# Agent attention and a mixture of experts on one core: an order set by step numbers replaced by a list scheduler in the kernel

## Chip, cores and metric

One core of a Trainium2 chip. The metric is the device time of one execution in microseconds (us). The kernel before was run twice: 1181.36 and 1184.54, median 1182.95 us.

## The reference

For each of B = 4 batches there are N = 11456 tokens of 128 values and 49 agents. The agents attend to the keys, which gives 49 agent values; each query attends to the agents and mixes these values. The 45824 rows x go through a top-1 mixture of 8 experts.

```python
a2k = softmax(scale * agents @ k.T)          # 49 x N
agent_v = a2k @ v                            # 49 x 128
x = softmax(scale * q @ agents.T) @ agent_v  # N x 128
logits = x @ w_gate                          # 8 experts
e = argmax(logits); gate = softmax(logits)[e]
out = gate * (relu(x @ w1[e]) @ w2[e])       # w1: 128 x 1024, w2: 1024 x 128
```

## The kernel before

A batch has 12 chunks: eleven of 1024 tokens (128 partitions x 8) and one of 192. Values in fp32 are split into an fp16 high and low part, and a product is then three fp16 matmuls.

*Keys* of a chunk: load, sum of squares on ACT (`squares`, L330), a power-of-two scale from its bits with three small DVE operations (`scale_bits`, L211, L215, L218), high part on ACT and low part on DVE (`split`, L346, L348), a DMA transpose from SP (`turn_over`, L370), the scores on PE (L397 to L399), evicted by L413 or L415, and a running maximum (L434). In the first batch the keys are instead transposed by PE in fp32 and scored by fp32 matmuls (`transposed`, L385; L395). After the last chunk come the column maximum (`keymax`, L439 to L451), then per chunk the subtraction (`kexp`, L459), the exponential (L464), its sum on POOL or DVE (`kexp3`, L474) and the product with v (`values`, L487). Small work follows: agent values, the batch's main expert (`choose`), the loads of its two weights, the folding of agent values into the first weight (L700), scales and splits (`weights`). `pow2_scale` (L180) is PE and DVE in turn, emitted at once.

*Queries* of a chunk: the same split, transpose and scores, then maximum, subtraction (L576, L578) and exponential (L583), the exponentials' split into the tile `mm` (L590, L594), a DMA transpose into M (`eturn`, L600), the routing logits (`logits`, L609 to L613) and, for groups of two or three chunks, the routing (`route`, L628 to L655).

*Experts.* All tokens of a batch go through the batch's most likely expert, in 23 groups of up to 512 tokens x 8 slices of 128 hidden values: 184 steps. A step is a first layer (two matmuls of 512 columns, L1171 and L1172), a relu on ACT (L1177), the low part on DVE (L1178), and five steps later (`LAG`) a second layer of twelve matmuls (L1191). The hidden part waits in four PSUM buffers and eight SBUF tiles. Each group is scaled and stored (L1204).

*Leftovers.* Tokens of other experts are ranked (`leftover_ranks`, on POOL, in the last batch on DVE), gathered by indirect DMAs into 14 blocks of 128 (`prepare_blocks`), and run with their own weights after the last batch (`block_layer1`, `block_layer2`). `weight_squares` (L884) loads all 16 expert weights for their scales. A loop behind that would run blocks that are still left.

*What orders the work.* A heap of events. Each function is put at a time in units of expert steps, by constants at the top (L45 to L64): `at(t, f)` and `after(dt, f)`. Steps of the experts stand at 184 b + i. The events are taken in order of time and each emits what its function holds, for all engines it uses:

```python
at(base + t + kl, kscores, c)
at(base + tl, logits, c)
after(NDL, weight_squares2, j, x)        # the square, 4 steps behind its load
```

Keys of the next batch start at step -208 of that batch, ten steps apart, its values four steps apart, and its queries at -20, 8 to 13 steps apart; so both overlap in the first part of a batch. Loads are issued three uses ahead (`AHEAD`). An engine takes its instructions in the order emitted, so each of them can hold up what stands behind it. `hold` (L919) makes a small tile on DVE that the next relu takes as its bias (L1175).

## Time and profile before

| | |
|---|---|
| median of 2 runs | 1182.95 us |
| profiled execution, its own time | 1182.58 us |
| its span, first to last instruction | 1180.9 us |
| PE busy | 1049.1 us (89%) |
| PE weight loads busy (beside PE) | 839.2 us (71%) |
| DVE busy | 981.8 us (83%) |
| ACT busy | 754.1 us (64%) |
| POOL busy | 142.2 us (12%) |
| granted TensorE clock, mean | 0.952 |

PE is the matmul engine, DVE the vector engine, ACT the scalar engine, POOL is GpSimd and SP only issues DMAs. L12 is line 12 of the kernel. A granted clock of 1 is 2.4 GHz, of 0.5 is 1.2 GHz. "<-" behind an idle time names what ended it; "issue" means that nothing in the profile did.

### The profile page before, as it was taken

To read this page: it belongs to the slowest core of one execution; us is meant where nothing else is said; L and a number is where in the kernel's file an instruction comes from. 1 tells how busy PE (TensorE), PEld (TensorE's weight loads), DVE (VectorE), ACT (ScalarE), POOL (GpSimd) and SP (SyncE) were. 2 spreads that over 40 slices of the span, in tenths; PEclk is the share of its full clock that TensorE was granted. 3 is DMA by queue.
4 is the path that set the end of the run, shared out by engine and by line. 5 is a ranking of instruction groups with operands and counts; after the bars stand their busy time and mean duration, and the time that the engine had idled before them with its cause. 6 is when DMAs were issued, how large, how long until landed. Compare 5 with 4: busy or idle time off the path is not lost.

```text
span 1180.9 us, 34788 instructions
## 1 busy us (share of the span) xinstructions
PE 1049.1 (89%) x14206; PEld 839.2 (71%) x14206; DVE 981.8 (83%) x2442; ACT 754.1 (64%) x1338; POOL 142.2 (12%) x193
## 2 busy tenths in 40 slices
PE   8747799899998899799988989899989789999995
PEld 8726577677776777677776768677767677667895
DVE  3668899797788999698787999697789798799985
ACT  4548785574486886574486777574576556666682
POOL 0200000043000000042100000042000112110123
PEclk9858899999998999899998999999999999899998
DMA  8599988631299899741399998741365545423270
GB/s 328 208 208 244 226 201 209 162 110 47 85 266 210 184 234 226 190 118 41 100 263 220 179 230 204 179 102 49 108 166 117 117 101 133 142 79 130 66 273 14
DMA packets 265666, 190.94 MB, mean 162 GB/s; under 512 B 217513, under 2 KB 230306, under 8 KB 265504
## 3 DMA queue, kind: packets, MB, share of 16 engines
q1 hardware_dynamic: 263648, 185.39, 61.6%
q0 software_dynamic: 1568, 2.25, 1.1%
q8 instruction: 112, 1.84, 0.6%
q10 hardware_dynamic: 288, 1.05, 0.3%
q14 instruction: 50, 0.41, 0.1%
HBM read 99.75 MB, written 36.43 MB: 115 GB/s over the span
## 4 chain that ended last, share of the span: by engine, by line
PE 24%; DVE 17%; issue 7%; DMA 7%; ACT 5%; POOL 2%; POOLq 0%; SPq 0%; ACTq 0%; DVEq 0%
PE py L1191 11%; DVE hh L1178 7%; PE ph L1171 4%; PE ph L1172 4%; DMA M<-mm 3%; DMA ld<-in_q_dram 2%; ACT hh L1177 2%; DMA wn<-in_moe_w_dram 1%; POOL out_dram L1073 1%; DVE S L459 1%; PE ps_small L487 1%; ACT jk L330 1%; DVE wsp L1032 1%; DVE yo L1204 1%; DVE hl L348 1%
## 5 line engine op out<-in xcount | busy, mean ns | idle before, releaser
L1191 PEld LDWEIGHTS <-hh 128*128 128x128 f16 x8640 | 554.8, 100 | 174.0 <-issue 12.7
L1191 PE MATMUL py<-w2h,hh 128*128 128x128 f16 (+1 forms) x5760 | 614.4, 221 | 3.2 <-DVE E L578 2.2
L1177 ACT ACTIVATE hh<-ph 128x512 f16<-128x512 f32 (+1 forms) x728 | 414.4, 585 | 252.7 <-PE ph L1172 232.2
L1178 DVE SCALAR_TENSOR_TENSOR hh<-ph,hh 128x512 f16<-128x512 f32 (+1 forms) x736 | 482.4, 669 | 87.7 <-ACT hh L1177 83.2
L1191 PE MATMUL py<-w2l,hh 128*128 128x128 f16 (+1 forms) x2880 | 529.9, 221 | 0.9 <-issue 0.9
L1171 PE MATMUL ph<-M,Ah 128*128 128x512 f16 (+1 forms) x736 | 282.2, 384 | 27.4 <-DVE hh L1178 21.0
L1172 PE MATMUL ph<-M,Al 128*128 128x512 f16 (+1 forms) x736 | 281.5, 383 | 0.2 <-issue 0.2
L348 DVE SCALAR_TENSOR_TENSOR hl<-ld,mul,hl 128x1024 f16<-128x1024 f32 (+1 forms) x84 | 102.3, 1219 | 3.8 <-ACT hl L346 3.3
L346 ACT ACTIVATE hl<-ld,mul 128x1024 f16<-128x1024 f32 (+1 forms) x84 | 91.2, 1092 | 10.1 <-DVE mul L215 9.9
L1172 PEld LDWEIGHTS <-Al 128*128 128x128 f16 x736 | 73.1, 99 | 31.3 <-issue 30.6
L330 ACT ACTIVATE jk<-ld 128x1024 f16<-128x1024 f32 (+1 forms) x84 | 84.7, 1008 | 14.6 <-DMA ld<-in_q_dram 11.5
L1171 PEld LDWEIGHTS <-Ah 128*128 128x128 f16 x736 | 74.2, 101 | 12.0 <-issue 9.4
L594 POOL TENSOR_TENSOR mm<-E,mm 128x392 f16<-128x392 f32 (+1 forms) x18 | 18.2, 1011 | 527.0 <-DVE mm L590 494.9
L397 PE MATMUL ps_s<-agh,hT 128*128 128x49 f16 x572 | 54.8, 187 | 14.7 <-DMA hT<-hl 10.1
L397 PEld LDWEIGHTS <-hT 128*128 128x128 f16 (+1 forms) x630 | 53.6, 99 | 17.4 <-DMA hT<-hl 14.7
L1204 DVE TENSOR_TENSOR yo<-py,cs 128x512 f32<-128x512 f32 (+1 forms) x92 | 61.4, 668 | 2.3 <-PE ps_s L609 2.3
L398 PEld LDWEIGHTS <-hT 128*128 128x128 f16 (+1 forms) x630 | 52.6, 99 | 5.0 <-issue 4.4
L398 PE MATMUL ps_s<-agl,hT 128*128 128x49 f16 x572 | 54.4, 186 | 0.3 <-DVE agl L319 0.3
L399 PE MATMUL ps_s<-agh,hT 128*128 128x49 f16 x572 | 54.2, 186 | 0.0
L399 PEld LDWEIGHTS <-hT 128*128 128x128 f16 (+1 forms) x630 | 52.2, 99 | 0.5 <-issue 0.4
L583 ACT ACTIVATE E<-E,ln,div 128x392 f32<-128x392 f32 (+1 forms) x48 | 33.3, 694 | 26.1 <-DVE E L578 25.1
L474 POOL TENSOR_TENSOR es<-es,S 128x392 f32<-128x392 f32 (+1 forms) x39 | 42.5, 1091 | 23.3 <-ACT S L464 16.6
(296 smaller groups left out, 1253.3 us busy)
## 6 DMA issues: line engine op xcount, KB each, us to landing
ld<-in_k_dram SPq DMA_DIRECT2D x44, 512.0 KB
ld<-in_v_dram SPq DMA_DIRECT2D x44, 512.0 KB
ld<-in_q_dram SPq DMA_DIRECT2D x44, 512.0 KB
out_dram<-yo SPq DMA_DIRECT2D x88, 256.0 KB
w1e<-in_moe_w_dram SPq DMA_DIRECT2D x17, 512.0 KB
w2e<-in_moe_w_dram SPq DMA_DIRECT2D x17, 512.0 KB
exps<-E SPq DMA_DIRECT2D x44, 196.0 KB
wn<-in_moe_w_dram SPq DMA_DIRECT2D x16, 512.0 KB
```

The source lines that it names most:

```text
L330: nc.scalar.activation(jk[:p, :t * D], x[:p, :t, :].rearrange("p t d -> p (t d)"), AF.Square, accum_out=ss[:p])
L346: nc.scalar.activation(hi[:p, :t, :], x[:p, :t, :], AF.Copy, scale=m)
L348: nc.vector.scalar_tensor_tensor(lo[:p, :t, :], x[:p, :t, :], m, hi[:p, :t, :], op0=ALU.mult, op1=ALU.subtract)
L397: nc.tensor.matmul(o, x[:, 0, i, :p], AG["h"], start=True, stop=False)
L398: nc.tensor.matmul(o, x[:, 0, i, :p], AG["l"], start=False, stop=False)
L399: nc.tensor.matmul(o, x[:, 1, i, :p], AG["h"], start=False, stop=True)
L1171: nc.tensor.matmul(ph[:, :nn], st['Ah'][:, f, :], m, start=True, stop=False)
L1172: nc.tensor.matmul(ph[:, :nn], st['Al'][:, f, :], m, start=False, stop=True)
L1177: nc.scalar.activation(hh[:, 0, :nn], ph[:, :nn], AF.Relu)
L1178: nc.vector.scalar_tensor_tensor(hh[:, 1, :nn], ph[:, :nn], 0.0, hh[:, 0, :nn], op0=ALU.max, op1=ALU.subtract)
L1191: mm_ = lambda l, r, **k: nc.tensor.matmul(o, l, r, skip_group_check=True, **k)
L1204: nc.vector.tensor_tensor(yo[:p, :n, :], py[:p, :n * D].rearrange("p (i d) -> p i d", d=D), cs.unsqueeze(2).broadcast_to([p, n, D]), op=AL ...
```

## The change

Every piece of work becomes an entry for one engine, with a rank (its old step number, roughly), a cost in us, the entries that it needs, and the buffers that it takes and frees. `Plan.order` walks a clock over PE, DVE, ACT, POOL and SP: whenever an engine is free, the entry with the lowest rank whose needs are done and whose buffers are free goes next. DMAs go through one modelled queue (`move`) and land after `land`. Pools in `strict` are taken in order of rank. DVE entries other than those of experts and blocks get 8 added to their rank. The order that comes out is emitted as it is.

Beside it: of a chunk's scale, the first operation stays on DVE and the two others go to POOL; the sums of two logits become one reduction; routing has 12 DVE operations instead of 14; in the first batch every second key chunk is scaled by one power of two for all its partitions and scored in fp16; 13 load buffers instead of 11, 4 split tiles instead of 6; the weights to be squared go into load buffers, ten steps ahead; 2 query chunks instead of 3 are made before the first experts; the first batch's exponentials are summed on DVE but for the first; the held tiles are gone. The arithmetic of experts and blocks is unchanged.

```diff
-LDB, HLB, SPB, MP, HP, NH, NY = 11, 6, 14, 6, 8, 4, 2
+LDB, HLB, SPB, MP, HP, NH, NY = 13, 4, 14, 6, 8, 4, 2
...
+class Plan:
+    LATE = dict(DVE=0.12, ACT=0.14, PE=0.1, POOL=0.14, SP=0.1)
...
+        while len(out) < len(self.all):
+            while future and future[0][0] <= t + 1e-9:
+                e = heapq.heappop(future)[2]
+                ready[e["eng"]].append(e)
+            did, soon = False, float("inf")
+            for g in engines:
+                if busy[g] > t + 1e-9:
+                    continue
+                best = None
+                for e in ready[g]:
+                    when = can(e, t)
...
+                    if best is None or (e["rank"], e["n"]) < (best["rank"], best["n"]):
+                        best = e
...
+                busy[g] = t + e["cost"]
+                end = t + e["cost"] + (0.0 if e["move"] else self.LATE[g])
+                if e["move"]:
+                    begin = max(t + 0.4 * e["cost"], queue[0])
+                    queue[0] = begin + e["move"]
+                    end = max(end, queue[0]) + e["land"]
...
+        def scales(src, c):
+            p, hb = P if uniform(src, c) else chunks[c][1], SC[src, c]
+            mul = two.tile([P, 1], F32, tag="s" + src + "m", name="mul", bufs=6)
+            nc.gpsimd.tensor_scalar(mul[:p].bitcast(I32), hb[:p], -1.0, float(204 << 23), op0=ALU.mult, op1=ALU.add)
+            div = two.tile([P, 1], F32, tag="s" + src + "d", name="div", bufs=6)
+            nc.gpsimd.tensor_scalar(div[:p].bitcast(I32), hb[:p], AG["bits"][:p, :1], None, op0=ALU.add)
...
+            m = SC[src, c][0][:, :1]
+            if eng == "A":
...
+                nc.scalar.activation(TT[src, c][:, 0, h:h + n, :p], pv, AF.Copy, scale=m)
+            else:
...
+                nc.vector.scalar_tensor_tensor(xT[:, 1, h:h + n, :p], pv, m, xT[:, 0, h:h + n, :p],
+                                               op0=ALU.mult, op1=ALU.subtract)
...
-            lg = two.tile([P, 8, E + 1], F32, tag="lg", name="lg")
-            pv = ps[:p, :t * E2].rearrange("p (t e) -> p t e", e=E2)
-            nc.vector.tensor_copy(lg[:p, :t, :], pv[:, :, E + 1:])
-            nc.vector.tensor_tensor(RT["L"][:p, c * 8:c * 8 + t, :], pv[:, :, :E + 1], lg[:p, :t, :], op=ALU.add)
+            pv = QP.pop(c)[:p, :t * E2].rearrange("p (t j e) -> p t e j", j=2, e=E + 1)
+            nc.vector.tensor_reduce(RT["L"][:p, c * 8:c * 8 + t, :], pv, axis=AX.X, op=ALU.add)
...
-            nc.vector.tensor_scalar(se, d, 0.0, float(E), op0=ALU.is_lt, op1=ALU.mult)
-            nc.vector.tensor_tensor(se, se, eb, op=ALU.add)
-            yield
-            nc.vector.tensor_reduce(lm, se, axis=AX.X, op=ALU.min)
+            nc.vector.scalar_tensor_tensor(se, d, 0.0, eb, op0=ALU.is_ge, op1=ALU.mult)
+            nc.vector.tensor_reduce(lm, se, axis=AX.X, op=ALU.max)
...
-            nc.vector.tensor_scalar(rk, rk, 1e-9, None, op0=ALU.add)
-            nc.vector.reciprocal(rk, rk)
-            nc.vector.tensor_tensor(g, g, rk, op=ALU.mult)
+            nc.vector.scalar_tensor_tensor(g, rk, 1e-9, g, op0=ALU.add, op1=ALU.mult)
+            nc.vector.reciprocal(g, g)
...
+            add(n_("scaling", *x), base + t + d[1], "POOL", 0.33, scales, *x, r=[n_("hb", *x)],
+                take=[("sc" + src, n_(*x))])
+            add(n_("upper", *x), base + t + d[2], "ACT", 1.0 * u + 0.1, upper, *x, r=[n_("scaling", *x)], take=[("hl", n_(*x))])
+            add(n_("lower", *x), base + t + d[3], "DVE", 1.15 * u + 0.1, lower, *x, r=[n_("upper", *x)], free=[("ld", n_(*x))])
+            add(n_("turn", *x), base + t + d[4], "SP", 2.9 if u == 1 else 2.4, turn_over, *x, r=[n_("lower", *x)], take=[("hT" + src, n_(*x))],
+                free=[("hl", n_(*x))], land=1.3, move=3.0 if u == 1 else 0.8)
...
+            add(n_("kexp", c), base + t, "DVE", 0.5, kexp, c, r=[n_("keymax", 4)], head=None if first else head(t - HEAD))
...
+                    (eturn, 10, "SP", 1.25, None, dict(take=[("M", n_("q", c))], free=[(m_, n_("q", c))], land=1.3, move=1.5))):
...
+            add(n_("logits", c), base + tl, "PE", 0.22, logits, c, r=[n_("eturn", c), av(10)], take=[("s", n_("l", c))])
...
+                add(("L1", i), i, "PE", 0.432 * u, layer1, g, f, r=[(b, "eturn", c), (b, "fl", 0), (b, "fl", 1), ("L1", i - 1) if i else None],
+                    take=[("H", ("h", i))], free=([("M", (b, "q", c))] if lastc else []) + ([("W", (b, "A"))] if last_ else []))
+                add(("up", i), i + 0.3, "ACT", 0.49 * u, upper, g, f, r=[("L1", i)], take=[("hh", i)])
+                add(("lo", i), i + 0.6, "DVE", 0.6 * u + 0.02, lower, g, f, r=[("up", i)], free=[("H", ("h", i))])
+                add(("L2", i), i + LAG + 0.5, "PE", 0.67 * u, layer2, g, f, r=[("lo", i), (b, "sl"), ("L2", i - 1) if i else None], free=[("hh", i)],
+                    take=[("Y", (b, g))] if f == 0 else [])
...
+        add(("wn", j), t - 10, "SP", 0.4, weight_squares, j, take=[("ld", ("wn", j))], land=2.2, move=1.3, head=("L1", t - 14))
+        add(("wn2", j), t, "ACT", 1.3, weight_squares2, j, r=[("wn", j)], free=[("ld", ("wn", j))])
...
+    with tc.manual_schedule():
+        for e in plan.order():
+            e["f"](*e["a"])
```

## Rows read from the trace of the kernel before

**Rows 1.** Windows by stage: us, busy (x instructions) per engine, PEclk, DMA share, GB/s.
```profile
0.00:85.00 85.00, 57.26 (x555) 52.70 (x555) 46.49 (x141) 38.06 (x68) 9.76 (x24) 0.80 0.78 249
85.00:359.50 274.50, 247.21 (x3377) 193.38 (x3378) 230.66 (x557) 185.17 (x327) 26.04 (x42) 0.94 0.71 173
359.50:622.20 262.70, 241.29 (x3373) 189.91 (x3370) 225.59 (x544) 178.90 (x316) 28.45 (x43) 0.97 0.73 174
622.20:882.10 259.90, 237.47 (x3317) 186.66 (x3314) 222.69 (x537) 172.68 (x304) 29.01 (x42) 0.98 0.67 159
882.10:1122.10 240.00, 221.51 (x2885) 173.36 (x2882) 215.70 (x601) 147.28 (x275) 30.24 (x28) 0.98 0.43 112
1122.10:1180.90 58.80, 44.34 (x719) 43.15 (x717) 40.68 (x67) 32.04 (x51) 18.66 (x14) 0.94 0.42 143
```

**Rows 2.** First line of the first layer: durations min/median/max ns, first and last start.
```profile
L1171 PE MATMUL ph<-M,Ah x736: 242/379/634, 85.0 to 1122.1; 128*128 128x512 f16 x176, 128*128 128x192 f16 x8
```

**Rows 3.** Chain that ended last: start us, us, what.
```profile
456.26 0.67 PE py L1191 x12
457.36 0.67 PE py L1191 x12
...
655.88 6.36 DMA M<-mm
```

**Rows 4.** Waits, whole span: waited for, us in total, times, longest us.
```profile
ACT jk L895 <- DMA wn<-in_moe_w_dram: 26.9, 11, 6.0
...
PE ph L1171 <- DVE hh L1178: 21.0, 15, 3.9
...
PE ps_s L609 <- DMA M<-mm: 20.1, 11, 3.6
...
PE ps_s L397 <- DMA hT<-hl: 10.1, 8, 1.8
...
PE ps_small L190 <- DVE pdg L188: 7.2, 6, 3.2
...
PE ps_small L442 <- DVE m L439: 7.1, 4, 2.6
```

**Rows 5.** Timeline, a stall in the second batch: start us, us [idle before <-releaser].
```profile
479.94 10.18 SPq L890 DMA_DIRECT2D wn<-in_moe_w_dram  x3
...
483.73 1.06 ACT L895 ACTIVATE jk<-wn 128x1024 f16<-128x1024 f32 x1 [6.05 <-DMA wn<-in_moe_w_dram]
...
485.40 2.48 DVE L1178 SCALAR_TENSOR_TENSOR hh<-ph,hh 128x512 f16<-128x512 f32 x4 [6.99 <-ACT hh L1177]
486.14 0.58 PE L1171 MATMUL ph<-M,Ah 128*128 128x512 f16 x1 [3.89 <-DVE hh L1178]
```

**Rows 6.** Groups by form: xcount, busy us, mean ns, idle before.
```profile
L218 DVE TENSOR_SCALAR div<-hb,bits 128x1 int32<-128x1 int32 x77 | 15.5, 203 | 0.0
...
L215 DVE TENSOR_SCALAR mul<-hb 128x1 int32<-128x1 int32 x81 | 11.8, 145 | 0.4
...
L612 DVE COPY lg<-ps_s 128x72 f32<-128x72 f32 x39 | 8.7, 223 | 6.9 <-PE ps_s L609 6.9
...
L820 POOL TENSOR_TENSOR cp<-cp,C 128x8 f32<-128x8 f32 x36 | 7.4, 206 | 2.8
```

**Rows 7.** Source of a routing line: min/median/max ns.
```profile
L631 DVE TENSOR_SCALAR sel<-Ld x20: 185/243/424, 85.0 to 1047.6; 128x192 f32<-128x192 f32 x8, 128x64 f32<-128x64 f32 x4, 128x128 f32<-128x128 f32 x4, 128x144 f32<-128x144 f32 x4
```

**Rows 8.** Groups by form: key scores of the first batch, fp32.
```profile
L395 PE MATMUL ps_y<-agf,xT 128*128 128x49 f32 x96 | 12.0, 280 | 0.0
...
L395 PE MATMUL ps_s<-agf,xT 128*128 128x49 f32 x80 | 9.4, 271 | 0.0
```

**Rows 9.** Timeline of PE over one fp16 score chunk, first matmul and what follows.
```profile
453.96 0.19 PE L397 MATMUL ps_s<-agh,hT 128*128 128x49 f16 x1
...
454.57 0.38 PE L1171 MATMUL ph<-M,Ah 128*128 128x512 f16 x1
```

**Rows 10.** Source of the key subtraction: min/median/max ns.
```profile
L459 DVE TENSOR_TENSOR S<-S,mxb x48: 246/594/1385, 41.4 to 786.0; 128x392 f32<-128x392 f32 x44, 96x98 f32<-96x98 f32 x4
```

More of the change, by code (lines that the diff above doesn't have):

```diff
@@ L426, in kmax @@
             sv = S[c][:p, :t, :]
-            if PKM and not first:
-                return
             if c == 0:
@@ new lines, in attention @@
+        add(n_("agload"), base + (KS - 20 if not first else -400) if b != 1 else base - steps - 8, "SP", 0.4, agent_load, land=1.5, move=0.1,
+            take=[("ag", n_())], head=head((KS if b > 1 else KS1 - base) - 14) if not first else None)
+        ka = -400 if first else KS - 8 if b > 1 else KS1 - base - 6
+        add(n_("agscaled"), base + ka, "DVE", 0.3, agent_scaled, r=[n_("agload")])
+        add(n_("agsquares"), base + ka + 0.1, "ACT", 0.5, agent_squares, r=[n_("agscaled")])
+        add(n_("agsum"), base + ka + 0.2, "PE", 0.4, agent_sum, r=[n_("agsquares")], take=[("s", n_("ag"))], free=[("ag", n_())])
@@ L1008, in prepare_blocks @@
         nc.vector.tensor_tensor(gt, gt, div[:, :n], op=ALU.mult)
+        yield
         for i in range(n):
```

1045 lines of the change are left out of this document (663 added, 382 removed).

## Prediction

> **What bounds the kernel now.** I read the windows by stage first, then the groups for the price of one piece of work, then the waits for what breaks the pace, then one break in the timeline.
>
> The first expert matmul starts at 85.0 us, the last at 1122.1 [rows 2]. So there are three stages: a head of 85 us, a steady part of 1037.1 us with 736 expert steps in four batches, and a tail of 58.8 us with the 14 leftover blocks. In the steady part PE is busy for 247.2 + 241.3 + 237.5 + 221.5 = 947.5 us and idle for 89.6 [rows 1]. DVE is busy for 230.7 + 225.6 + 222.7 + 215.7 = 894.7 us, that is 86%. Two engines are thus both near the limit. Undisturbed, a step costs 1.10 us: the twelve second-layer matmuls of one step start at 456.26, those of the next at 457.36, back to back [rows 3]. So PE sets the pace where nothing breaks it.
>
> Two things break it. One is the 89.6 us of PE idle time. The other is the granted clock: it averages 0.94, 0.97, 0.98 and 0.98 over the four batches [rows 1], and since its levels are 1 and 0.5, the half-speed time is 2 x (0.06 x 274.5 + 0.03 x 262.7 + 0.02 x 259.9 + 0.02 x 240.0) = 69 us. Work done at half speed takes twice as long, so that is 34.4 us lost. Together 124 us of the steady part are not work at full speed. The idle time by cause [rows 4]: the first layer waiting for DVE to free a PSUM buffer 21.0 us, the logits waiting for the transposed exponentials M 20.1, the scores waiting for the transposed tokens 10.1, small helper matmuls waiting for DVE 7.2 + 7.1. That is 65.5; 24.1 us are spread over others.
>
> How such a stall is made is seen at 480 us [rows 5]. SP issues three weight loads from 479.94 on. ACT stands at the sum of squares of the first of these for 6.05 us, until it has landed. The relu of the expert steps is queued behind it, DVE is idle for 6.99 us because it needs that relu, and PE for 3.89 us because DVE frees its buffers. Then the matmuls run at half clock. Nothing was short: the order was wrong by some microseconds. ACT lost 26.9 us to these loads in eleven waits [rows 4].
>
> **The change part by part.** *The order.* Before, every piece of work stands at a hand-set step, and a piece that spans engines (a helper matmul and the DVE work before and behind it) is emitted at once, wherever its input is. After, each piece is for one engine, is put in the queue only when the plan's clock says that its inputs and buffers are there, and has the loads and transposes in that clock. What I expect of each cause:
> - The loads for the squares now go out ten steps (11 us at 1.10) ahead of their use instead of four, into the load buffers. Landing took about 4 us in rows 5. The stalls of that kind go. The expert DVE work now has first rank, and all other DVE work is ranked eight steps later. Of the 21.0 us I take 13 off, as the plan can't split a long DVE piece.
> - Helpers: the PE matmul is put in only when its DVE input is planned to be ready, with experts between. Of 14.3 us I take 10 off.
> - M and token transposes: the plan books 1.5 us on a shared queue and 1.3 us to land for M, after 0.4 of its 1.25 us issue, 3.3 us in an empty queue. One in the trace took 6.36 us [rows 3], so the plan is early unless its queue is as full as the real one. Of 20.1 + 10.1 I take half, 15 off.
> - The other 24.1 us: a third, 8 off.
>
> Together 46 of 89.6 us, 51%. The half clock follows stalls (rows 5), so I take the same 51% of 34.4 us: 17.6. Sum of the order: 63.6 us.
>
> *What the order gives back.* Its prices are low in places. The key subtraction is booked at 0.5 us; the median in the trace is 0.594 and the longest 1.385 [rows 10], so 44 full ones cost 4 to 39 us more DVE time than planned. Four expert steps in PSUM and eight hidden tiles cover a DVE that is late by a few microseconds, no more. I charge 12 us, nearer to the low end since the median is the usual case; the ends are 0 and 39.
>
> *Scales on GpSimd.* Per chunk two DVE operations go, 0.203 + 0.145 us [rows 6], 84 chunks in all, and two POOL operations come; six key chunks of the first batch are new and get them as well. The nearest POOL row is 0.206 us for 128x8 [rows 6], so 90 x 0.41 = 37 us on an engine that has 28 of 263 us busy in a batch. DVE saves 84 x 0.348 = 29 us. The added wait stands in front of the ACT scaling of a chunk, behind which relus queue, and DVE and PE wait for these. POOL is in order too: a scale that meets one of the rank pieces (planned at up to 4.4 us) waits for it. The plan books both on POOL, so ACT should get other work in between; if not, each meeting costs as much as the stall of rows 5. The POOL time is hidden beside PE, the DVE time counts only where DVE is last, and I give it no term of its own: it is what lets the order above find room.
>
> The key subtraction takes 0.594 us in the median and up to 1.385 [rows 10], in stretches where POOL adds the exponentials of the chunk before. The Trainium skill (GPSIMD Engine Reference, Key points) has a rule for it that speaks against moving anything there: GpSimd shares its SBUF interfaces with VectorE and contends with DVE instructions that have two SBUF inputs. If all 37 us of new POOL time stretched such DVE operations in that ratio of 2.3, DVE would lose 37 x (1 - 1/2.3) = 21 us, and by that the time would be up to 21 us longer than my sum; the new operations have one element per partition.
>
> *One sum for the logits.* Two DVE operations of 0.223 us (the copy of rows 6 and an add alike) become one reduction over 144 elements; between the copy and the two together I take 0.30, so 0.15 x 44 = 6 us. *Routing:* of 14 DVE operations per span two go, 0.243 [rows 7] and one shorter, at most 0.45 together, x 20 spans = 8 to 9 us. With the scales DVE loses about 43 us, 10 or 11 per batch: 225.6 becomes 215. In a batch that is shorter by 15 us (248) that is still 87%, the share of now. So DVE does not become idle; it stays as near to the limit as it is.
>
> *Half of the first keys in fp16.* A chunk of fp32 scores costs PE (12.0 + 9.4) / 11 = 1.95 us [rows 8]; in fp16 the 24 matmuls take 0.61 [rows 9]. Six chunks save 8 us of PE in the head. Squares, sums, scales and splits come to ACT and DVE, which have 38 and 46 of 85 us busy [rows 1]; the first chunk's chain is late by some 3 us. Between 0 and 8 I take 5. The small DVE work between the agent values and the first expert weights no longer queues behind chunk splits: 2 us. Head: 7 us.
>
> *Two load buffers more, two split buffers fewer, first queries 2 instead of 3, sums of the first exponentials on DVE, the held tiles gone:* each is under 3 us by its rows' size and they go both ways; I take 0. *Tail:* the same 48 matmuls a block in the same sequence, POOL and PE as before: 0, bounds -5 and +5.
>
> The sum: 1182.58 us is the profiled execution (span 1180.9 and 1.7 around it), which stands 0.4 below the median of the runs. 1182.6 - 63.6 + 12 - 7 = 1124 us. With the taken shares between a third and two thirds it is 1095 to 1150.
>
> **The rivals.** *The order is nearly right everywhere (1085).* For it: the pace of 1.10 us without a gap over many steps in the chain [rows 3] shows that nothing else is needed. Then three quarters of 89.6 + 34.4 go, 93, with 7 in the head and little given back: about 1083 to 1085. Against it: DVE at 86% and a DMA whose pieces take twice the planned time.
>
> *Only the arithmetic counts (1168).* The new order has stalls of its own in the same number; the head's 7 us and some 8 of DVE's 43, in the share in which the first layer waits for DVE (21.0 of 89.6 us of idle time, less what ACT causes), remain: 1168. For it: prices fixed by hand stand in both. Against it: rows 5, a stall that the new order can't make in that form.
>
> *The landing of M decides, and it is slower (1215).* PE is in order: a logits matmul put in front of experts before its M has landed stops all. Now this happens in 11 waits at 20.1 / 11 = 1.8 us. If the plan's 3.3 us against 6.4 makes it happen to all 44 full chunks, that is 81 us, 60 more; with the clock's 0.38 us per us of idle time 83. The other gains are left (7 in the head, (13 + 10 + 8) x 1.38 = 43): 83 - 50 = 33 slower, 1215. It decides from about 60 us of waits for M and transposed tokens on PE. For it: DMA is 0.71 and 0.73 busy over the first two batches [rows 1], and the transposes do not lie evenly in them. Against it: the plan has a queue of its own that gets late with load, and logits are ranked five steps behind their transpose.
>
> **How the numbers follow.** The forecast has 0.53, the very good order 0.18, only arithmetic 0.17, the late landings 0.12. A measurement of this kernel can tell about 2%: faster is below 1159.3, slower above 1206.6. Faster holds the first two and a quarter of the third: 0.75. Slower is the last, less what of it stays below 1206: 0.10. The rest, 0.15, is no change. The range reaches from the very good order to a little above only-arithmetic: 1082 to 1174; the slow rival is left out.
>
> **What would show it.** Right: ACT's waits for the weight loads near 0; PE's idle time in the steady part about 45 to 60 us; clock 0.97 or more in each batch; the first expert matmul at 76 to 80 us; no scale operations on DVE and DVE busy by some 30 to 40 us less, POOL's busy time near 180; batches of 245 to 252 us. Wrong: PE waiting for M or transposed tokens for more than 60 us, ACT waiting for POOL in front of a scaling, or DVE idle more than now while PE waits for it.

## The result: 1148.7 us, and the profile after

The changed kernel ran twice: 1148.67 and 1148.70 us, against 1182.95 before. The ratio is 0.971, with an interval from 0.965 to 0.977. So it is faster by 2.9%, and 24.7 us slower than the forecast of 1124. In a later session the same kernel beside the same kernel before gave 0.972 (0.965 to 0.979). In the later sessions some runs of the kernel before, and one of the kernel with the new arithmetic alone, took 2 to 3% longer than the others of the same kernel; the ratios and times given here go by the others.

The windows by stage of the changed kernel, cut as in [rows 1] at the first expert matmul of each batch and at the last one (columns: us; busy us of PE, PE's weight loads, DVE, ACT and POOL; granted clock; DMA share; GB/s):

```profile
0.00:82.90 82.90, 53.48 (x565) 48.23 (x565) 53.37 (x163) 39.44 (x72) 7.52 (x34) 0.76 0.57 200
82.90:331.40 248.50, 237.47 (x3391) 185.91 (x3392) 225.91 (x468) 183.72 (x324) 43.45 (x91) 0.98 0.79 193
331.40:574.10 242.70, 235.57 (x3367) 184.60 (x3367) 221.53 (x479) 177.95 (x317) 42.85 (x91) 1.00 0.78 190
574.10:817.40 243.30, 232.98 (x3319) 182.28 (x3319) 219.44 (x469) 173.48 (x305) 41.09 (x89) 1.00 0.72 174
817.40:1071.70 254.30, 227.34 (x2902) 174.85 (x2902) 225.34 (x554) 148.87 (x279) 31.18 (x45) 0.96 0.47 120
1071.70:1146.90 75.20, 49.50 (x720) 48.20 (x717) 47.19 (x86) 35.58 (x55) 19.98 (x18) 0.82 0.33 102
```

Read beside [rows 1], stage by stage: the head went from 85.0 to 82.9, the first three batches from 274.5, 262.7 and 259.9 to 248.5, 242.7 and 243.3, which is 62.6 us less. Then it turns round. The last batch went from 240.0 to 254.3 and the tail from 58.8 to 75.2: 30.7 us were given back. In the three batches PE idles 28.5 us (71.1 before) and the clock is 0.98 or more. In the last batch it fell from 0.98 to 0.96, in the tail from 0.94 to 0.82.

The waits of PE, which answer to [rows 4] (waited for, us in total, times, longest):

```profile
PE ph L1465 <- DVE hh L1477: 26.5, 22, 3.1
PE ps_small L531 <- DMA hT<-hl: 12.6, 13, 5.7
PE ps_small L758 <- DMA M<-mm: 9.7, 11, 1.3
PE pyb L1351 <- ACT hh L1337: 6.4, 2, 4.1
```

Before, some of the logits and scores stood under a second tile name, in two lines that [rows 4] leaves out:

```profile
PE ps_y L609 <- DMA M<-mm: 6.8, 2, 6.6
PE ps_y L397 <- DMA hT<-hl: 1.8, 1, 1.8
```

With them the waits for M went from 26.9 to 9.7 us. Those for transposed tokens went from 11.9 to 12.6, but 5.7 of the 12.6 are one wait in the head. The first layer's wait for DVE has grown from 21.0 to 26.5, and its place has changed: in the first three batches it fell from 16.9 to 9.2, in the last one it rose from 4.3 to 17.3. ACT's wait for the squared weights [rows 4] fell from 26.9 to 1.8 us. In front of the chunk's scaling ACT now waits for GpSimd where it waited for DVE, about as long (the first line is before, the second after):

```profile
ACT hl L346 <- DVE mul L215: 9.9, 12, 1.9
ACT hl L470 <- POOL mul L462: 10.8, 14, 3.2
```

### The profile page after: what moved, and what is told of

The parts are those of the page before. It is cut to its first block, busy times and chain, and to the rows that moved or that the text cites. A ratio compares the mean times of both kernels' runs of the same rounds, so it can differ in the third digit from the quotient of the medians.

```text
span 1146.9 us, 34925 instructions
## 1 busy us (share of the span) xinstructions
PE 1036.3 (90%) x14260; PEld 824.1 (72%) x14260; DVE 992.8 (87%) x2213; ACT 759.0 (66%) x1350; POOL 186.1 (16%) x367
## 3 DMA queue, kind: packets, MB, share of 16 engines
q1 hardware_dynamic: 263648, 185.39, 63.6%
## 4 chain that ended last, share of the span: by engine, by line
PE 53%; DVE 19%; DMA 16%; issue 8%; ACT 3%; POOL 1%; SPq 0%; POOLq 0%; ACTq 0%; DVEq 0%
PE py L1490 25%; PE ph L1465 8%; PE ph L1466 8%; DMA hT<-hl 7%; DVE hh L1477 7%; DMA M<-mm 4%; PE ps_small L618 3%; DMA ld<-in_q_dram 2%; ACT hh L1472 1%; PE ps_small L531 1%; PE ps_acc L618 1%; DMA ld<-in_k_dram 1%; DVE wsp L1321 1%; DVE hl L475 1%; PE ps_small L533 1%
## 5 line engine op out<-in xcount | busy, mean ns | idle before, releaser
L1490 PEld LDWEIGHTS <-hh 128*128 128x128 f16 x8640 | 536.1, 99 | 146.8 <-issue 14.8
L1490 PE MATMUL py<-w2h,hh 128*128 128x128 f16 (+1 forms) x5760 | 595.5, 220 | 4.4 <-DVE yo L1499 1.9
L1490 PE MATMUL py<-w2l,hh 128*128 128x128 f16 (+1 forms) x2880 | 520.4, 220 | 0.7 <-issue 0.7
L1477 DVE SCALAR_TENSOR_TENSOR hh<-ph,hh 128x512 f16<-128x512 f32 (+1 forms) x736 | 472.0, 668 | 50.3 <-ACT hh L1472 47.6
L1465 PE MATMUL ph<-M,Ah 128*128 128x512 f16 (+1 forms) x736 | 277.0, 377 | 30.0 <-DVE hh L1477 26.5
L462 POOL TENSOR_SCALAR mul<-hb 128x1 int32<-128x1 int32 (+1 forms) x90 | 27.7, 308 | 494.5 <-DVE hb L455 477.4
L436 ACT ACTIVATE jk<-ld 128x1024 f16<-128x1024 f32 (+1 forms) x90 | 90.5, 1006 | 18.6 <-DMA ld<-in_q_dram 9.3
L470 ACT ACTIVATE hl<-ld,mul 128x1024 f16<-128x1024 f32 (+1 forms) x84 | 91.0, 1093 | 12.8 <-POOL mul L462 10.8
L531 PE MATMUL ps_small<-agh,hT 128*128 128x49 f16 (+1 forms) x630 | 58.5, 186 | 13.0 <-DMA hT<-hl 12.6
L531 PEld LDWEIGHTS <-hT 128*128 128x128 f16 (+1 forms) x630 | 51.6, 98 | 22.6 <-DMA hT<-hl 19.9
L533 PE MATMUL ps_small<-agh,hT 128*128 128x49 f16 (+1 forms) x630 | 58.1, 185 | 0.0
L532 PE MATMUL ps_small<-agl,hT 128*128 128x49 f16 (+1 forms) x630 | 58.1, 185 | 0.0
L532 PEld LDWEIGHTS <-hT 128*128 128x128 f16 (+1 forms) x630 | 50.9, 98 | 2.5 <-issue 0.6
L533 PEld LDWEIGHTS <-hT 128*128 128x128 f16 (+1 forms) x630 | 50.6, 97 | 0.0
L605 POOL TENSOR_TENSOR es<-es,S 128x392 f32<-128x392 f32 (+1 forms) x33 | 35.0, 1060 | 61.7 <-ACT S L595 61.0
L728 ACT ACTIVATE E<-E,ln,div 128x392 f32<-128x392 f32 (+1 forms) x48 | 33.0, 687 | 16.6 <-DVE E L723 15.8
```

The source lines that it names most:

```text
L436: nc.scalar.activation(jk[:p, :t * D], x[:p, :t, :].rearrange("p t d -> p (t d)"), AF.Square, accum_out=ss[:p])
L470: nc.scalar.activation(hl[:p, 0, :t, :], loaded[b, src, c][:p, :t, :], AF.Copy, scale=SC[src, c][0][:p, :1])
L531: nc.tensor.matmul(o, x[:, 0, i, :p], AG["h"], start=True, stop=False)
L532: nc.tensor.matmul(o, x[:, 0, i, :p], AG["l"], start=False, stop=False)
L533: nc.tensor.matmul(o, x[:, 1, i, :p], AG["h"], start=False, stop=True)
L1465: nc.tensor.matmul(ph[:, :nn], st['Ah'][:, f, :], m, start=True, stop=False)
```

## The experiments

All numbers by stage come from windows cut in the same way, from one profile of each kernel. How far two profiles of one kernel can lie apart is seen in the second and third line of the table: 6.6 us in the last batch, 3.2 in the head. The total times have their intervals.

The runs are from several chips, and the totals move with them. The kernel before took 1181.4 us in the median beside the arithmetic alone, the scales on DVE, the stores and the gathers, about as in the first session, but 1171.4 to 1172.5 beside all the others, and on one of those chips the changed kernel took 1139.1 instead of 1148.7. So up to some 10 us between two lines of the table, or between a time and an expectation that was counted from 1148.7, can be the chip's. Where it matters the ratio decides, since it has the kernel before on the same chip.

| kernel | head | batch 1 | 2 | 3 | 4 | tail | batches 1 to 3 | 4 and tail |
|---|---|---|---|---|---|---|---|---|
| before | 85.0 | 274.5 | 262.7 | 259.9 | 240.0 | 58.8 | 797.1 | 298.8 |
| changed | 82.9 | 248.5 | 242.7 | 243.3 | 254.3 | 75.2 | 734.5 | 329.5 |
| changed, later session | 79.7 | 248.4 | 242.5 | 242.7 | 247.7 | 76.5 | 733.6 | 324.2 |
| before, new arithmetic alone | 81.3 | 273.1 | 263.6 | 263.1 | 245.4 | 59.0 | 799.8 | 304.4 |
| new order alone | 80.6 | 254.4 | 247.6 | 248.4 | 260.1 | 76.6 | 750.4 | 336.7 |
| changed, scales on DVE | 80.6 | 252.4 | 242.3 | 246.6 | 254.9 | 77.1 | 741.3 | 332.0 |
| changed, first keys whole | 82.2 | 255.4 | 246.9 | 245.0 | 243.5 | 75.4 | 747.3 | 318.9 |
| stores first | 80.5 | 247.0 | 248.6 | 240.2 | 244.2 | 85.4 | 735.8 | 329.6 |
| gathers' landing | 78.8 | 248.0 | 243.1 | 242.3 | 248.1 | 77.1 | 733.4 | 325.2 |
| late splits | 80.5 | 248.1 | 241.7 | 242.2 | 248.3 | 75.7 | 732.0 | 324.0 |
| all three | 79.1 | 251.8 | 243.2 | 238.4 | 233.9 | 80.1 | 733.4 | 314.0 |
| and six output buffers | 79.2 | 245.1 | 245.2 | 238.3 | 234.5 | 77.1 | 728.6 | 311.6 |
| and two prices | 80.2 | 240.0 | 239.4 | 235.2 | 237.6 | 76.6 | 714.6 | 314.2 |
| and splits between relus | 80.0 | 239.9 | 240.4 | 235.0 | 237.2 | 73.0 | 715.3 | 310.2 |

### Order and arithmetic apart

*The arithmetic alone, on the old order.*

```diff
-        nc.vector.tensor_scalar(mul[:p, :n].bitcast(I32), hb[:p, :n], -1.0, float((190 + to) << 23),
+        eng = nc.vector if bits is None else nc.gpsimd
+        eng.tensor_scalar(mul[:p, :n].bitcast(I32), hb[:p, :n], -1.0, float((190 + to) << 23),
...
-            nc.vector.tensor_copy(lg[:p, :t, :], pv[:, :, E + 1:])
-            nc.vector.tensor_tensor(RT["L"][:p, c * 8:c * 8 + t, :], pv[:, :, :E + 1], lg[:p, :t, :], op=ALU.add)
+            pv = ps[:p, :t * E2].rearrange("p (t j e) -> p t e j", j=2, e=E + 1)
+            nc.vector.tensor_reduce(RT["L"][:p, c * 8:c * 8 + t, :], pv, axis=AX.X, op=ALU.add)
...
-            nc.vector.tensor_scalar(se, d, 0.0, float(E), op0=ALU.is_lt, op1=ALU.mult)
-            nc.vector.tensor_tensor(se, se, eb, op=ALU.add)
+            nc.vector.scalar_tensor_tensor(se, d, 0.0, eb, op0=ALU.is_ge, op1=ALU.mult)
...
```

> The kernel before with its own order, plus only the arithmetic of the change: one sum for the logits, the shorter routing, the scales of the token chunks on GpSimd. My theory: the gain is the order's; this alone gives 1178 us (1170 to 1184), VectorE about 40 us less busy, TensorE's idle time in the four batches still above 80 us. Rival: the arithmetic carries most of the gain: 1148 to 1162, with TensorE's idle time falling to 60 us. Second rival: the GpSimd hop sits on the written order's path: slower, 1186 to 1200.

Measured: 1187.21 us, ratio 1.007 (1.004 to 1.010). DVE was 17.7 us less busy (964.1 instead of 981.8), and nothing came of it. PE's waits show where it went (same columns as above):

```profile
PE ps_s L612 <- DMA M<-mm: 30.7, 12, 4.5
PE ph L1170 <- DVE hh L1177: 14.6, 21, 4.7
PE ps_y L612 <- DMA M<-mm: 5.1, 2, 2.8
```

The first layer waits less for DVE (14.6 instead of 21.0), and the logits wait more for M (35.8 instead of 26.9). As I read it, on the old order a faster DVE only reached the next wait sooner. The forecast of 1178 was too hopeful, and the rival of 1148 to 1162 fell. The time lies in the range of the second rival, that the way over GpSimd costs something; but ACT waits 8.0 us for GpSimd's scales here and waited 9.9 for DVE's, so that wait doesn't show its mechanism.

*The order alone, with the old arithmetic.* The same lines turned back in the changed kernel, with the scales planned on DVE at 0.35 us. The buffers' numbers, the first keys in halves and the other small edits of the change stay in, so "order" means the order and these:

```diff
-            nc.gpsimd.tensor_scalar(mul[:p].bitcast(I32), hb[:p], -1.0, float(204 << 23), op0=ALU.mult, op1=ALU.add)
+            nc.vector.tensor_scalar(mul[:p].bitcast(I32), hb[:p], -1.0, float(204 << 23), op0=ALU.mult, op1=ALU.add)
...
-            add(n_("scaling", *x), base + t + d[1], "POOL", 0.33, scales, *x, r=[n_("hb", *x)],
+            add(n_("scaling", *x), base + t + d[1], "DVE", 0.35, scales, *x, r=[n_("hb", *x)],
...
-            add(n_("logits2", c), base + tl + 0.6, "DVE", 0.25, logits2, c, r=[n_("logits", c), n_("logits2", c - 1) if c else None],
+            add(n_("logits2", c), base + tl + 0.6, "DVE", 0.45, logits2, c, r=[n_("logits", c), n_("logits2", c - 1) if c else None],
...
```

> The changed kernel with the arithmetic of before (two operations for the logits, the longer routing, scales on VectorE), planned at matching prices: the order alone. The arithmetic on the old order was worth nothing (0.7% slower), and the scales alone on the new order some 8 us. If the list order alone carries the gain: 1155 to 1168 us, the first three batches together 742 to 755 us (734.5 with the whole change, 797.1 before). Rival: order and arithmetic need each other; 1170 to 1185, three batches 765 or more.

Measured: 1169.79 us, ratio 0.998 (0.996 to 1.0005). Neither part is worth anything alone; together they are worth 2.9%. The windows of this run say where the two meet:

```profile
80.60:335.00 254.40, 239.58 (x3392) 188.09 (x3393) 234.79 (x541) 184.78 (x325) 27.57 (x43) 0.98 0.79 189
335.00:582.60 247.60, 236.87 (x3370) 185.19 (x3369) 231.35 (x546) 177.98 (x316) 27.64 (x43) 0.99 0.74 185
582.60:831.00 248.40, 234.48 (x3319) 183.59 (x3319) 230.01 (x537) 172.19 (x303) 27.19 (x43) 0.99 0.72 172
831.00:1091.10 260.10, 230.04 (x2902) 178.12 (x2902) 230.72 (x591) 150.45 (x279) 26.71 (x25) 0.95 0.46 115
```

In the three batches the order alone takes off 46.7 us (797.1 to 750.4), and in the last batch and the tail it loses 37.9 (336.7 against 298.8). With the head that would leave a gain of 13.2 us where the ratio leaves 2, so some 11 us of these differences belong to the chip or the session; in which stages isn't known, since the kernel before was profiled once. DVE is now 234.8 of 254.4 us busy, 92%, and 93% in the next two batches, and PE waits more for it than in the changed kernel (40.6 us against 26.5):

```profile
PE ph L1469 <- DVE hh L1481: 40.6, 36, 3.3
```

So the new order has run into DVE. The arithmetic takes 16 us more off the three batches and 7.2 to 12.5 off the rest. Expected was 1155 to 1168 or, for the rival, 1170 to 1185. By its ratio, 0.998 of 1182.95 or 1181 us, the total is the rival's, while the three batches lie in my range. What I called the order's gain needs the arithmetic to come out.

*The scales alone back on DVE.*

> The changed kernel, with the two scale operations of each token chunk back on VectorE (planned there at 0.35 us). My theory: the move to GpSimd is worth little, VectorE gains some 12 us of work that lies beside TensorE: 1150 us (1145 to 1157), ScalarE's 10.8 us of waits for the GpSimd multiplication gone. Rival 1: the move is the main gain: 1165 to 1180. Rival 2: the hop over GpSimd costs more than it saves: 1138 to 1145.

Measured: 1158.87 us, ratio 0.983 (0.978 to 0.987), so about 1.1 points lost against the changed kernel's 0.971 and 0.972; the intervals just meet. DVE is 19.6 us busier (1011.8 against 992.1 in the later session's run). So the scales carry some two fifths of the 2.7 points that the arithmetic brings on the new order, and the single sum and the routing, by difference, the rest. The expected 1150 was too low: the scales on GpSimd are worth more than I thought, though not the 16 us or more of the first rival. And ACT's waits were not GpSimd's doing: it waits 8.9 us for the same tile from DVE.

*The first keys whole in fp32* (`SPLIT0 = (False,)`).

> The changed kernel with the first batch's keys all in fp32, as before the change, and none split into halves in the head. The prediction put 5 us of the head's gain on the halves. If so: the first expert matmul at 85 to 89 us and 1151 to 1156 in all. Rival: the halves bring nothing since the head waits for loads and for the chain of key maxima: first matmul at 79 to 83 us, 1145 to 1150.

Measured: 1149.88 us with runs from 1141.5 to 1156.7, ratio 0.981 (0.974 to 0.988). The first expert matmul starts at 82.2, with the halves at 78.8 to 82.9 in eleven profiles, 80.2 in the median. So the halves bring about 2 us in the head, not 5, which is nearer to the rival. The total is a point above the changed kernel's, with intervals that overlap; if it is real, it lies in the batches, isn't explained by the head and stays open.

### The last batch and the tail

Three things stood out in the changed kernel's trace. In the last batch DVE waits for gathered ranks that the scheduler had booked to land after 1.5 us (timeline of DVE: start us, us, what, and in brackets the idle time before it):

```profile
876.98 2.48 DVE L1477 SCALAR_TENSOR_TENSOR hh<-ph,hh 128x512 f16<-128x512 f32 x4
883.47 0.17 DVE L1231 TENSOR_TENSOR fr<-tsl,fg 128x4 f32<-128x4 f32 x1 [4.02 <-DMA fg<-ranks,fri]
```

In the tail ACT takes nine weight splits in a row, with four relus queued behind them (timeline of ACT):

```profile
1093.32 1.15 ACT L1318 ACTIVATE wsp<-w2e,tsm 128x1024 f16<-128x1024 f32 x1 [3.46 <-PE ph L1332]
1094.37 1.13 ACT L1318 ACTIVATE wsp<-w1e,tsm 128x1024 f16<-128x1024 f32 x1
...
1101.65 1.14 ACT L1318 ACTIVATE wsp<-w2e,tsm 128x1024 f16<-128x1024 f32 x1
1102.69 2.02 ACT L1337 ACTIVATE hh<-ph 128x512 f16<-128x512 f32 x4
```

And the stores of both stages, which free the two accumulators of the second layer, fall under the rule that puts DVE work 8 steps back. Each was mended by itself.

*The stores first.*

```diff
-        if name[0] not in ("lo", "up", "bd", "bu", "L1", "L2"):
+        if name[0] not in ("lo", "up", "bd", "bu", "L1", "L2", "bs") and name[1] != "store":
```

> The changed kernel, with the two stores of the tail (the last groups' output stores and the blocks' stores on VectorE) ranked like the lower halves instead of 8 steps later. My theory: the tail's extra 16 us (75.2 us after 1071.7, where it was 58.8) comes in good part from these stores: they come late on VectorE, hold the two layer-2 accumulators, and the blocks' second layers start late. Expected 1140 us (1135 to 1145), the last stretch 63 to 70 us long instead of 75.2, the four batches unchanged. Rival 1: the bursts of weight splits alone hold the tail; then 1147 to 1150 and a last stretch of 73 to 76 us. Rival 2: the early stores push lower halves back in the batches too, and the kernel is slower, 1150 to 1158 with more PE idle before layer 2.

Measured: 1143.0 us, ratio 0.968 (0.963 to 0.972), not told apart from the changed kernel. The tail is longer (85.4 us), which no theory had said, and the last batch shorter (244.2; 247.7 and 254.3 without the edit); the two together are 329.6, as before the edit. My reading of the tail fell: the late stores alone are not its cause.

*The gathers' landing*, 4.5 us instead of 1.5 at both gathers.

```diff
...
-                ("POOL", 4.2 * z, dict(land=1.5, move=0.3)),
+                ("POOL", 4.2 * z, dict(land=4.5, move=0.3)),
```

> The changed kernel, with the scheduler told that the two kinds of gathers land after 4.5 us instead of 1.5. My theory: the last batch became 14 us longer because VectorE, which takes its instructions in order, stands 4 us at the operation that needs the gathered ranks, with lower halves queued behind it, and the matmul clock falls after it. Expected 1142 us (1138 to 1147), the last batch 246 to 250 us instead of 254.3, no VectorE wait over 2 us for the gather. Rival: the last batch is long since the sheer amount of preparation work on VectorE stands in it (225 us busy of 254); then the time stays at 1147 to 1150 with the idle time moved elsewhere.

Measured: 1139.39 us, ratio 0.967 (0.962 to 0.972), not told apart from the changed kernel. The last batch came out at 248.1, in my range, and DVE's waits for the gather were gone. It seemed a hit until the changed kernel itself was profiled again: with 9.9 us of these waits still in it, its last batch had 247.7.

```profile
DVE fr L1231 <- DMA fg<-ranks,fri: 9.9, 3, 4.3
```

The wait was real, and by itself it cost nothing that can be seen.

*The late splits*, ranked beside the block that they run ahead of.

```diff
-            add(("wu",) + x, t + FS + (FWJ if u < WA else 3) * j / 2, "ACT", 1.1, weights_split, u, j, True,
+            ts = t + FS + (FWJ - 2) * j / 2 if u < WA else B * steps + 2.4 * (u - WA) + 7 + 0.2 * j
+            add(("wu",) + x, ts + j, "ACT", 1.1, weights_split, u, j, True,
...
```

> The changed kernel, with the weight splits of the last seven blocks ranked beside the block that they run ahead of (2.4 us a block) instead of up to 20 us before it. My theory, after the stores alone moved nothing: the tail's bubbles are the bursts of splits on ScalarE and VectorE, with the blocks' relus behind them. Expected 1140 us (1135 to 1145), the last stretch 63 to 69 us instead of 75.2, no more than 8 us of TensorE idle in it before the last matmul (15 us now). Rival: the bursts come since buffers for splits come free all at once, whatever the rank; then 1146 to 1151 and the last stretch stays at 73 to 77 us.

Measured: 1139.82 us, ratio 0.973 (0.969 to 0.977), the tail 75.7. The time is in my range only because of the chip; by the ratio and the tail nothing changed, as the rival had it. But the edit hardly moved the splits: on ACT seven of them still stand in a row, where there were nine. So it tested neither theory of the bursts; the last run of this section does.

*All three*, the edits above in one kernel.

> The changed kernel, with all three repairs at once: gathers priced to land after 4.5 us, late splits ranked beside their blocks, stores ranked like the lower halves. If the three causes are separate and add: 1128 to 1135 us, the last batch and the tail together 310 to 315 us (329.5 now, 298.8 before the change). Rival: last batch and tail share one limit, and what leaves one comes back in the other, as in the run with the stores alone; then 1137 to 1145 and 322 to 330 us for the two together.

Measured: 1125.72 us, ratio 0.961 (0.957 to 0.964), below the changed kernel's interval. The last batch and the tail are 314.0 together, in the first theory's range, where the repeated changed kernel has 324.2 and each edit alone 324.0 to 329.6. By the ratio, 1136 us on the first chip, the total lies between the two forecasts. Against 0.971 the three edits alone gained 0.3, 0.4 and nothing, and together 1.0 points. It may be that each hid behind the others, or that two small gains simply add: the intervals, half a point either way, don't tell, and no pair was run.

```profile
812.50:1046.40 233.90, 218.03 (x2877) 171.22 (x2877) 218.64 (x522) 149.99 (x280) 30.73 (x44) 0.99 0.47 123
1046.40:1126.50 80.10, 49.41 (x723) 47.83 (x720) 52.66 (x117) 35.12 (x56) 20.99 (x18) 0.88 0.35 109
```

The last batch is now shorter than before the change (240.0 in [rows 1]) at a clock of 0.99. The tail is not.

*Six output buffers.* In that tail DVE stood at a block's store until an earlier block's output had left through GpSimd's queue; the two buffers of these outputs are no resource of the scheduler's.

```profile
DVE yb L1358 <- DMA out_dram<-yb,fti: 6.0, 2, 4.8
```

```diff
-        yo = bh[u, "yo"] = two.tile([P, D], F32, tag="yb", name="yb")
+        yo = bh[u, "yo"] = two.tile([P, D], F32, tag="yb", name="yb", bufs=6)
```

> The kernel with the three repairs, and six buffers instead of two for the blocks' scaled outputs, which leave through GpSimd's queue. In the three repairs' tail VectorE stood 4.8 us at a block's store, until an earlier block's output had left, and then 12 weight splits came in a row ahead of the lower halves, with TensorE 5.2 us idle. My theory: the buffers set this off; expected 1117 us (1113 to 1121), the tail 70 to 73 us instead of 79.6, no wait of VectorE for an output. Rival: the burst of splits comes from the written order, and the tail keeps its length, 78 to 81 us, 1123 to 1128.

Measured: 1123.14 us, ratio 0.958 (0.953 to 0.963). The wait is gone, the tail lost 3 us (77.1), and the burst of splits was still there: between the two theories, nearer to the rival, and not told apart in total.

*The splits between the relus.* The same splits once more, ranked 4 us ahead of their own block, on DVE without the 8 steps. This one was tried on top of the two prices of the next section.

```diff
-            ts = t + FS + (FWJ - 2) * j / 2 if u < WA else B * steps + 2.4 * (u - WA) + 7 + 0.2 * j
+            ts = t + FS + (FWJ - 2) * j / 2 if u < WA else B * steps + 2.4 * u - 4
+            td = ts if u < WA else ts - DX
...
```

> The kernel with the repairs, buffers and prices, and the late weight splits ranked once more: a block's splits 4 us before that block's own first layer, and on VectorE without the 8 steps' delay, so that relus of earlier blocks go ahead of them. Until now they were ranked up to 10 us too early for that: in the two last runs with the splits beside the blocks, bursts of them still stood ahead of the relus, and TensorE lost 11 us in the tail to relus and lower halves of blocks. If the rank makes the bursts: the tail 68 to 72 us instead of 76.1 and 1104 to 1110 us in all. Rival: the buffers of the splits, which come free together, make them; then the tail stays at 74 to 78 and 1110 to 1116.

Measured: 1111.3 us, ratio 0.948 (0.945 to 0.952), beside 0.949 without it. The bursts were the rank's doing: relus and splits of the early blocks alternate now, as in this stretch of ACT,

```profile
1061.06 0.58 ACT L1337 ACTIVATE hh<-ph 128x512 f16<-128x512 f32 x1
1061.54 1.15 ACT L1318 ACTIVATE wsp<-w1e,tsm 128x1024 f16<-128x1024 f32 x1
1062.58 0.59 ACT L1337 ACTIVATE hh<-ph 128x512 f16<-128x512 f32 x1
1063.06 1.16 ACT L1318 ACTIVATE wsp<-w2e,tsm 128x1024 f16<-128x1024 f32 x1
```

PE's waits for relus of blocks are gone and the tail's clock is 0.91. But the tail is only 3.6 us shorter (73.0, just above my range), and the total, which lies in the rival's range, can't be told from the kernel without the edit. Up to the last matmul PE idles 13.4 us in this tail; without the edit it is 16.8, before the change 3.7. So the bursts explain little of what the tail lost. What is left, 14 us against [rows 1], isn't settled: PE waits there 5.3 us for splits on DVE and 3.0 us for the last group's preparation, and neither was tried.

### Two prices nearer to the trace

In the changed kernel's groups the two scale operations on GpSimd take 0.32 and 0.35 us, booked at 0.33 together (columns as in [rows 6]):

```profile
L464 POOL TENSOR_SCALAR div<-hb,bits 128x1 int32<-128x1 int32 x83 | 28.9, 348 | 0.0
...
L462 POOL TENSOR_SCALAR mul<-hb 128x1 int32<-128x1 int32 x83 | 26.4, 318 | 484.0 <-DVE hb L455 467.0 <-ACT hh L1472 12.3 <-DVE s L443 4.8
```

The edit books 0.65, and 2.3 us instead of 1.3 for the landing of both kinds of transposed tiles; nothing that is computed changes.

```diff
-            add(n_("scaling", *x), base + t + d[1], "POOL", 0.33, scales, *x, r=[n_("hb", *x)],
+            add(n_("scaling", *x), base + t + d[1], "POOL", 0.65, scales, *x, r=[n_("hb", *x)],
...
-                free=[("hl", n_(*x))], land=1.3, move=3.0 if u == 1 else 0.8)
+                free=[("hl", n_(*x))], land=2.3, move=3.0 if u == 1 else 0.8)
...
-                    (eturn, 10, "SP", 1.25, None, dict(take=[("M", n_("q", c))], free=[(m_, n_("q", c))], land=1.3, move=1.5))):
+                    (eturn, 10, "SP", 1.25, None, dict(take=[("M", n_("q", c))], free=[(m_, n_("q", c))], land=2.3, move=1.5))):
```

> The kernel with the three repairs and six output buffers, with two more prices set nearer to the trace: the pair of scale operations on GpSimd 0.65 us instead of 0.33, the landing of the transposed tiles 2.3 us instead of 1.3. The three batches still lose 16 us of 30 in waits for transposed tiles. If the price matters: 3 to 8 us less than the run with the buffers alone, TensorE's waits for transposed tiles halved. Rival: the transposes wait for the queues and not for a price, and the longer landing only moves the same work: within 3 us of it, or slower.

Measured: 1112.57 us, ratio 0.949 (0.944 to 0.954), 10.6 us less than with the buffers alone on the same chip, more than I expected. PE's waits for M and for transposed tokens, without the two prices and with them:

```profile
PE ps_small L531 <- DMA hT<-hl: 11.6, 8, 5.7
PE ps_small L758 <- DMA M<-mm: 8.3, 11, 1.5
...
PE ps_small L531 <- DMA hT<-hl: 6.9, 3, 5.7
PE ps_small L533 <- DMA hT<-hl: 2.2, 2, 1.9
PE ps_small L758 <- DMA M<-mm: 1.9, 5, 0.6
```

Those for M went from 8.3 to 1.9 us, those for tokens from 11.6 to 9.1, of which 5.7 is in both the one in the head. The three batches lost 14 us (728.6 to 714.6) and PE's idle time in them 11.6 (24.4 to 12.8), of which these waits are 9.6. I did not try the two prices apart. The rival fell: the prices, at least one of them, mattered.

### The changed kernel again

> The changed kernel as it is, beside the repaired ones on the same chip: 1140 to 1149 us, 0.971 of before within its interval, the last batch at 249 to 255 us and the tail at 75 us, so that the repaired kernels are told from it on one chip.

Measured: 1139.14 us where before had 1171.51, ratio 0.972 (0.965 to 0.979). The tail is 76.5. The repaired kernel with the two prices ran beside it at 0.949 (0.944 to 0.954): the intervals are apart, so it beats the kernel before by 5.1 points and the changed one by 2.3.

## Why the prediction was right in kind and 25 us off

The step that failed is the one word on the tail: "the same 48 matmuls a block in the same sequence, POOL and PE as before: 0, bounds -5 and +5". It measured +16.4 us (75.2 against 58.8), and 17.7 in the repeat. The matmuls are indeed the same; the splits, relus and stores between them are not, since the list puts whatever is ready by its rank, where the hand order took one pair of splits per block. Up to the last matmul PE idled 3.7 us in the tail before, all for DVE, and 15.0 after (the first line is before):

```profile
PE ph L1044 <- DVE hh L1049: 3.7, 5, 0.9
...
PE pyb L1351 <- ACT hh L1337: 6.4, 2, 4.1
PE pyb L1353 <- DVE hh L1341: 4.6, 2, 3.0
PE ph L1330 <- DVE hh L1341: 2.4, 1, 2.4
PE pyb L1351 <- DVE yb L1358: 1.6, 1, 1.6
```

That is 11.3 of the 16.4 us. The rest is that the same matmuls took 5.2 us more (49.5 against 44.3 busy), at a granted clock of 0.82 instead of 0.94. What made the waits stays open in good part: stores, splits and output buffers, each mended, left the tail at 73 us or more. I had not asked what the scheduler does with the stretch that had been written out by hand. By the spans the error is 24.6 us: 16.4 are here, 4.9 in the head and 3.3 in the steady part.

*The steady part.* Forecast -63.6 and +12, together -51.6; measured 1037.1 to 988.8, that is -48.3. The size is right, the place is not: -62.6 in three batches and +14.3 in the last one (+7.7 in the repeat, on a faster chip). PE's idle time there fell from 89.6 to 55.4 us, where 43.6 was forecast, or 55.6 with the 12 us charged. The clock term held: by the same sum, 2 x (0.02 x 248.5 + 0.04 x 254.3) / 2 = 15.1 us are lost, 16.8 forecast. By cause the agreement is partly luck. The prediction set waits of the whole span against the idle time of the steady part, and it missed the second name of M's waits. Counted in the steady part alone, M and tokens went from 34.7 to 16.6 us, 18.1 less where 15 was forecast. The wait for DVE's buffers, of which I took 13 off, grew by 5.5, and all of that growth is in the last batch. Helpers and the rest lost 21.6, forecast 18. The 12 us charged for low prices and a late DVE cover most of that miss of 18.5; that they had about the right size is luck.

*What the order needs.* I gave the saved DVE time no term, "it is what lets the order above find room". The sentence was right and the weight was missing: the order without it gave 0.998. On the new order 37.5 us of DVE time (1030.3 busy with the old arithmetic, 992.8 with the new) come with 2.7%, some 32 us. On the old order 17.7 us of it were worth nothing. The rival "only the arithmetic counts" fell with that run.

*DVE busy.* I wrote that DVE would be 30 to 40 us less busy; the page says 992.8, 11 more than before. Adding up the lengths of all DVE records gives 1147.4 us before and 1111.3 after, 36 less (the scales 29.2, the logits 7.1 and the routing 9.1 less; the first keys' new splits and the rest add 9 again). But records overlap on this engine, and busy time counts overlapping ones once: before, 165.6 us lay under another record, after, 118.6. Why the new order overlaps less isn't settled. So an operation's length was the wrong price for taking it away. For the scales, 90 chunks x 0.35 us of records moved and DVE's busy time changed by 19.6 us, 0.22 a chunk.

*The head.* Forecast -7, measured -2.1 and, in the repeat, -5.3; the halves 2 instead of 5.

*What the order gives back.* I charged 12 us for low prices, and two better prices brought 10.6. They are not the price that I had named, the key subtraction, which was never tried.

*The rivals.* The landing of M as what decides fell: PE's waits for M were 9.7 us, not 81. But it pointed at a price that was too low: with it and the scales' price set nearer to the trace these waits went to 1.9. The very good order was not reached; nearest to it comes the kernel with the two prices, which takes 82.5 us off the three batches (797.1 to 714.6, some of it the chip's) but keeps the long tail.

*The signs.* PE's idle time, the first three batches' clock, ACT's loads and GpSimd's busy time (186) came out as said. The first expert matmul at 82.9, three of the four batches outside 245 to 252, the last batch's clock of 0.96 and the busy time of DVE did not. Of the signs of being wrong one came: ACT waits for GpSimd in front of a scaling, 10.8 us. It means little, as ACT waited 9.9 there for DVE before.

*GpSimd's prices.* I took 0.206 us for one scale operation, 37 us in all; it was 0.32 and 0.35, 58.7 us in all. The rule of the Trainium skill that I weighed (GPSIMD Engine Reference, Key points) would have cost DVE up to 21 us: for the scales this trace shows none of it. The low half of the split, which reads two SBUF inputs, takes 1.23 us in the mean with the scales on GpSimd and 1.22 with them on DVE. It was GpSimd that waited for DVE there; behind longer GpSimd operations DVE waits, too (both below).

## What to carry to other kernels

A better order pays only until the next engine is full, and less work on an engine pays only where the order lets it count. Try both alone and together before either is given up: each alone was worth nothing here. When a scheduler replaces an order written by hand, look at every stretch the hand had tuned, the end above all, and set its prices from the trace early: two of them brought 10.6 us here, more than any single repair of ranks, although one for the gathers brought nothing by itself. Profile the same kernel twice before a wait in one stretch is called the cause.

## What was unexpected of the hardware

*Small DVE operations overlap.* In the kernel before, four scale operations start 0.06 to 0.12 us apart while their records have 0.14 to 0.20 us (timeline of DVE: start us, us, what):

```profile
450.13 0.15 DVE L215 TENSOR_SCALAR mul<-hb 128x1 int32<-128x1 int32 x1
450.20 0.20 DVE L218 TENSOR_SCALAR div<-hb,bits 128x1 int32<-128x1 int32 x1
450.32 0.14 DVE L215 TENSOR_SCALAR mul<-hb 96x1 int32<-96x1 int32 x1
450.38 0.20 DVE L218 TENSOR_SCALAR div<-hb,bits 96x1 int32<-96x1 int32 x1
```

A pair takes 0.19 us from start to start, not 0.35.

*A tiny GpSimd operation waits out a DVE operation.* The scale of one element per partition takes 0.19 us in the median and 1.22 at most. 15 of its 90 records are over 0.4 us, 10 us more than the median in all, and each of the 15 lies beside a DVE operation with two inputs in SBUF; the eight of 1.1 to 1.2 us all lie beside the low half of a split. One of them, DVE, POOL and ACT in turn (timeline of each):

```profile
382.14 1.27 DVE L475 SCALAR_TENSOR_TENSOR hl<-ld,mul,hl 128x1024 f16<-128x1024 f32 x1
...
382.25 1.22 POOL L462 TENSOR_SCALAR mul<-hb 128x1 int32<-128x1 int32 x1 [1.28 <-DVE hb L455]
...
383.49 1.15 ACT L470 ACTIVATE hl<-ld,mul 128x1024 f16<-128x1024 f32 x1 [1.01 <-POOL mul L462]
```

The scale starts behind the split, ends just after it, and ACT, which needs it for the next chunk, stands for a microsecond. It goes the other way round as well. The running maximum of the keys, two inputs in SBUF, takes 0.56 us on DVE in the median. It took 1.27 when a GpSimd operation with two SBUF inputs had started 0.06 us ahead of it, and it ended 0.4 us behind that one (timelines of POOL and DVE):

```profile
149.19 0.91 POOL L746 TENSOR_TENSOR mm<-E,mm 128x392 f16<-128x392 f32 x1
...
149.25 1.27 DVE L563 TENSOR_TENSOR mx<-mx,S 128x392 f32<-128x392 f32 x1
```

So does the key subtraction of [rows 10]: before, its ten longest, 1.38 us each, all started 0.2 to 0.3 us behind a sum on GpSimd and ended 0.4 us behind its end. The Trainium skill (SBUF — State Buffer, Who interferes with whom) says that a DVE instruction with two SBUF inputs contends with a GpSimd one that reads SBUF, and that the order in which they are issued decides which of them blocks. This trace agrees in both orders. A scale on GpSimd is over so soon, in 0.19 or 0.28 us, that being first it delays DVE little: the splits that started beside a scale already running took 1.27 to 1.30 us, as they do in the median (1.28).
